# A delta-rule recurrence with an MLP behind it: chunks 0 and 1 solved apart, pairs from chunk 2 on, another split of the first tiles, and the order of the work from a table

## The chip, the cores and the metric

The kernel runs on one core of a Trainium2 chip. The metric is the device time of the program in microseconds (us). Its engines are PE (TensorE, matrix products, with its weight loads shown as PEld), DVE (VectorE), ACT (ScalarE), POOL (GpSimd) and SP (SyncE, which here only issues transfers). ACT and POOL issue transfers too.

## The reference

Each of 4 x 8 heads carries a state of 48 x 48 through 768 tokens. Its readings are put together to 384 columns, and an MLP with a tanh GELU runs over the 3072 tokens.

```python
def _attn_ref(q, k, v, beta):           # (4, 8, 768, 48); beta (4, 8, 768)
    k_n = k / (np.linalg.norm(k, axis=-1, keepdims=True) + 1e-06)
    state = zeros(B, H, D, D)
    for t in range(S):
        y[:, :, t] = einsum('bhd,bhde->bhe', q[:, :, t], state)
        v_old = einsum('bhde,bhd->bhe', state, kt)
        state = state + bt * einsum('bhd,bhe->bhde', kt, vt - v_old)

def _moe_ref(x, w_in, w_out):           # x (3072, 384), w_in (384, 2048), w_out (2048, 384)
    h = x @ w_in
    g = 0.5 * h * (1.0 + tanh(c * (h + 0.044715 * h**3)))
    return g @ w_out
```

## The kernel before

**The recurrence by chunks.** The 768 tokens are cut into 12 chunks of 64 (`C`, `NCH`). 32 heads lie as 16 pairs, a head in each half of the 128 partitions. Inside a chunk the recurrence is a triangular system: its matrix comes from the Gram matrix of the normalized keys times beta, and its inverse T, applied to v minus what the state already holds, gives the update U. The steps of a chunk `c` are:

- `load`: SP fetches keys, values and queries (`kf`, `vf`, `qf`; a chunk's keys are two transfers of 192 KB).
- `prep`, `prep2`, `prepq`: squares, sums and norms of the keys (`sq`, `ss`, `sr`, `rn`), the normalized keys `Kn`, and their transposes with the queries' in `KQT`, by PE with the identity as one operand.
- `gram`: the 64 x 64 products K K^T and K Q^T of every head; the first goes to `G`, the second, masked with `mD`, to `DT`.
- `own`, `blocks`: the diagonal 16 x 16 blocks of the triangular system. `own` makes the products of 32 x 32, a vector transpose puts them into `Tt`, they are multiplied with beta and a mask (`bM`) into `Y`, and 14 rounds of a multiplication and an addition each (28 instructions, `tmp` and `Y`) solve all blocks at once. Then beta goes in twice (`XW`), and vector transposes bring the results back as `TB`.
- `inverse`: `WB` and `DI` spread the solved blocks over the 64 columns, and four products with what follows each (`WB,G` to `ET`; then `DI,ET`, and `TT,ET` twice, each to a part of `TT`) build the whole inverse.
- `state`: KS (keys times state S) and R = KS - v; `R,TT` to U; KU to the next S; QS and DU to the output `x`.

A unit of two chunks shares one `blocks`: (0,1) is solved on DVE, and (2,3), (4,5) and on are solved on POOL (`UNITS`, `eng = "pool" if u else "dve"`). All of the solve is in f32.

**The MLP by tiles.** `TILES` are [0], [1], then [2,3], [4,5] to [10,11]. A tile with one chunk is 4 batches x 64 = 256 tokens, one with two is 512. Layer one has 16 blocks of 128 hidden columns, each the sum of three products with 128 rows of the weights `W1`. The 384 columns of x come out of `state` as 4 groups of 2 x 48 rows, so a gather of six small transfers (`x<-x`, issued by SP) moves the fourth group into free rows of the other three. Tile 0 does without the gather: it reads a fourth weight tile `W4` that lies for this time in the last four buffers of `gT`. ACT applies the GELU into `gT`; layer two is four groups of two bursts of 8 products each, whose result goes by `osb` to the output.

**What sets the order.** The kernel records operations (`P.op`) with the engines that may run them, an estimated cost, what they read and write, and a priority. `Plan.schedule` then simulates the engines, the transfers and the fetching of instructions (`Fetch`), and takes the ready operation of the best priority on each engine; it also gives out the eight PSUM banks. `Plan.emit` writes one instruction stream for each engine in that order, with semaphore waits where a dependency crosses engines. So every engine is in order, and an instruction that waits holds up all behind it on its own engine. The same holds for the transfers in SP's and POOL's queues.

Lines that the prediction's steps use: L372 is the helper of every tensor_tensor, L377 of copies, L381 of activations, L388 of matmuls, L396 of transfers; L897 is the transpose into `Tt`; L907, L912 and L916 the solve; L923 and L928 `XW`; L936 the transposes back; L979 `WB` and `DI`; L633 the memset for the fourth weight tile.

Of the kernel before, what the change touches and what calls it, by code (L numbers as in the profile page):

```python
# [5 lines left out]
F32 = mybir.dt.float32  # L6
BF16 = mybir.dt.bfloat16
# [7 lines left out]
LAT = {"pe": 0.22, "dve": 0.06, "act": 0.06, "pool": 0.08, "sp": 0.0}  # L15
SWITCH = 0.095
SLACK = 0.3
URGENT = -100.0
CRIT, WAIT = -85.0, 0.9
EARLY_T, MARGIN = 55.0, (2.0, 1.0, 0.2)  # L20
COLD_T, COLD = 36.0, 1.3
BURST = 1.2
BANKS = {"t": (0, 6), "f": (6, 8), "l": (0, 8)}
NEAR = {"pe": 0.3, "dve": 0.1, "act": 0.05, "pool": 0.1, "sp": 0.0}


def turn(a, b):
    if a == b:
        return 0.0
    return SWITCH  # L30


class Fetch:

    BLOCK, FIRST, EVENTS = 256, 63, 1.0025
    TIMES = ((50.0, 6.5), (125.0, 4.5), (1e9, 3.7))

    def __init__(self):
        self.pos, self.ready = float(self.FIRST), 0.0

    def run(self, t, cost, n, keep=False):
        pos, ready = self.pos, self.ready
        left = n * self.EVENTS
        per = cost / left
        while left > 1e-6:
            k = min(self.BLOCK - pos % self.BLOCK, left)
            t += k * per
            pos += k
            left -= k
            if self.BLOCK - pos % self.BLOCK < 1e-6:  # L50
                pos = float(round(pos))
            if pos % self.BLOCK == 0:
                t = max(t, ready)
                ready = t + next(w for x, w in self.TIMES if t < x)
        if keep:
            self.pos, self.ready = pos, ready
        return t


class Op:  # L60
    __slots__ = ("idx", "cost", "fns", "deps", "prio", "alloc", "uses", "dma", "lat",
                 "eng", "start", "end", "count", "clock", "sync", "mode", "bw", "bk", "fence", "nm", "at")


class Plan:


# [12 lines left out]
    def op(self, cost, fns, reads=(), writes=(), prio=0.0, alloc=(), dma=None, lat=0.0, mode="s", bk="t", bw=0.0, nm=0,  # L80
           free=(), at=0.0):
        o = Op()
        o.idx = len(self.ops)
        o.cost, o.fns, o.prio, o.dma, o.lat, o.mode, o.bw, o.bk, o.nm = cost, fns, prio, dma, lat, mode, bw, bk, 2 * nm
        o.alloc, o.at = tuple(alloc), at
# [29 lines left out]
    def schedule(self):  # L115
        ops = self.ops
        succ = [[] for _ in ops]
        left = [len(o.deps) for o in ops]
        for o in ops:
            for d in o.deps:  # L120
                succ[d].append(o.idx)
        ready = {e: [] for e in ENGINES}

        def push(o):
            for e in o.cost:
                ready[e].append(o.idx)

        for o in ops:
            if left[o.idx] == 0:
                push(o)  # L130
        free_at = {e: 0.0 for e in ENGINES}
        pe_mode = "s"
        burst = 0.0
        fetch = Fetch()
        dma_free = w_free = 0.0
        queued = []
        bank_free = [0.0] * self.nbanks
        bank_last = [()] * self.nbanks
        done = [False] * len(ops)
        orders = {e: [] for e in ENGINES}  # L140

        def dep_time(o, e):
            t = o.at
            for d in o.deps:
                p = ops[d]
                m = 0.0
                if o.prio > URGENT and p.end < EARLY_T and p.eng != e:
                    m = MARGIN[0] if p.dma else MARGIN[1] if p.eng == "pool" else MARGIN[2]
                t = max(t, p.end + m + (p.lat if p.dma else (0.03 if p.eng == e == "pe" else LAT[p.eng])))
            return t  # L150

        def find_banks(n, t0, lo, hi):
            best = None
            for i in range(lo, hi - n + 1):
                ts = bank_free[i:i + n]
                if any(x is None for x in ts):
                    continue
                t = max(max(ts), 0.0)
                key = (max(t, t0), i)
                if best is None or key < best[0]:  # L160
                    best = (key, i, t)
            return best

        n_left = len(ops)
        dep_cache = {}
        users_left = {h: len(u) for h, u in self.users.items()}
        while n_left:
            pick = None
            for e in ENGINES:
                if not ready[e]:  # L170
                    continue
                best = None
                for i in ready[e]:
                    o = ops[i]
                    if (i, e) not in dep_cache:
                        dep_cache[(i, e)] = dep_time(o, e)
                    t = max(free_at[e], dep_cache[(i, e)])
                    bb = []
                    tb = 0.0
                    if o.alloc:  # L180
                        ok = True
                        taken = []
                        for h, n in o.alloc:
                            sv = [(k, bank_free[k]) for k in taken]
                            for k in taken:
                                bank_free[k] = None
# [1111 lines left out]
```

## Time and profile before

| | us |
|---|---|
| runs | 259.02, 259.03, 259.76; median 259.03 |
| span of the profiled execution | 258.6 |
| PE busy | 216.8 (84%) |
| PE weight loads busy | 143.3 (55%) |
| DVE busy | 160.3 (62%) |
| ACT busy | 145.1 (56%) |
| POOL busy | 127.7 (49%) |
| moved by transfers | 24.56 MB, mean 95 GB/s |

A profile shows one execution. Busy time is the time in which an engine runs at least one instruction of the kind; matmuls overlap, and their ends are modelled. A group of instructions is told by its line, its engine, the operation and the tiles that it writes and reads. Idle time in front of an instruction is put down to what released it; "issue" means that nothing in the profile shows what it waited for. The granted clock is the share of full speed at which PE may run.

### The profile page before, as it was taken

The page shows a single profiled execution, that of the slowest core. Times are in us where ns is not written, and L with a number is a line of the kernel's source. Part 1 is how long each engine was busy: PE and PEld are TensorE (multiplying, and loading weights), DVE is VectorE, ACT ScalarE, POOL GpSimd, SP SyncE. Part 2 cuts the span into 40 slices and gives each one's busy share as a digit, 9 for nine tenths or more (in the row PEclk, how much of TensorE's full clock was granted, in tenths as well). Part 3 has the DMA queues.
Part 4 walks back from the last instruction along what each step waited for, and adds up shares of the span by engine and source line. Part 5 has one row for each costly group of instructions (what it writes and reads, how often), then busy time and mean ns, then how long its engine had stood idle before and what let it go on. Part 6 is the DMA issues. An engine that isn't in the chain of part 4 may idle for free.

```text
span 258.6 us, 11905 instructions
## 1 busy us (share of the span) xinstructions
PE 216.8 (84%) x5416; PEld 143.3 (55%) x5446; DVE 160.3 (62%) x288; ACT 145.1 (56%) x244; POOL 127.7 (49%) x234
## 2 busy tenths in 40 slices
PE   0573455559998789999989989999999999999995
PEld 0352345547875676555656655656556554446462
DVE  5659777683857999986998679738976210001011
ACT  4587895226954776379830578732676506850600
POOL 8559998989058892789518860686000000000000
PEclk9999995556999979999999999999999999999999
DMA  7999799981298855840611404131100030002111
GB/s 131 209 159 220 139 180 169 193 159 37 51 167 195 202 111 111 186 86 23 124 48 67 96 17 81 35 74 63 56 18 5 3 109 30 0 3 82 39 49 72
DMA packets 66129, 24.56 MB, mean 95 GB/s; under 512 B 53216, under 2 KB 65600, under 8 KB 66080
## 3 DMA queue, kind: packets, MB, share of 16 engines
q1 hardware_dynamic: 58368, 15.26, 31.1%
q0 software_dynamic: 2752, 3.54, 8.8%
q10 hardware_dynamic: 4960, 5.02, 5.7%
q8 instruction: 42, 0.69, 1.2%
q14 instruction: 7, 0.06, 0.1%
HBM read 21.43 MB, written 4.72 MB: 101 GB/s over the span
## 4 chain that ended last, share of the span: by engine, by line
PE 41%; POOL 28%; DVE 15%; issue 4%; DMA 4%; SPq 3%; ACT 3%; POOLq 0%
PE ps L388 40%; POOL Yf L916 6%; POOL tmp L912 6%; POOL Kn L372 4%; POOL sq L372 4%; SPq L396 3%; POOL W L396 3%; DMA qf<-in_q_dram 2%; DVE TB L936 2%; DVE WB L979 2%; DMA kf<-in_k_dram 2%; POOL DT L372 2%; POOL Yf L907 1%; ACT gT L381 1%; DVE TT L372 1%
## 5 line engine op out<-in xcount | busy, mean ns | idle before, releaser
L381 ACT ACTIVATE gT<-ps 128x512 bf16<-128x512 f32 x96 | 55.6, 597 | 40.0 <-PE ps L388 37.9
L388 PE MATMUL ps<-x,W 128*128 128x512 bf16 (+1 forms) x306 | 67.4, 353 | 4.5 <-issue 2.5
L388 PE MATMUL ps<-W,gT 128*128 128x384 bf16 x384 | 66.9, 327 | 0.0
L388 PEld LDWEIGHTS ps<-W,gT 128*128 128x128 bf16 x384 | 35.8, 98 | 23.8 <-ACT gT L381 0.5
L377 DVE COPY osb<-ps 128x384 f32<-128x384 f32 x21 | 11.7, 556 | 53.8 <-PE ps L388 53.7
L388 PEld LDWEIGHTS ps<-x,W 128*128 128x128 bf16 x336 | 29.9, 99 | 24.6 <-ACT gT L381 1.0
L372 DVE TENSOR_TENSOR TT<-ps,DI 128x256 bf16<-128x256 f32 (+4 forms) x39 | 24.9, 644 | 13.1 <-PE ps L388 12.6
L381 ACT ACTIVATE KQT<-ps 128x1024 bf16<-128x1024 bf16 (+1 forms) x24 | 23.6, 984 | 12.9 <-PE ps L795 10.6
L916 POOL TENSOR_TENSOR Yf<-Yf,tmp 128x28 f32<-128x28 f32 (+6 forms) x70 | 24.6, 351 | 5.5
L912 POOL TENSOR_TENSOR tmp<-Yf 128x28 f32<-128x28 f32 (+6 forms) x70 | 23.8, 340 | 5.4
L388 PE MATMUL ps<-KQT 48*32 48x32 bf16 (+1 forms) x1152 | 20.1, 207 | 6.8 <-DVE tmp L912 2.9
L381 ACT ACTIVATE G<-ps 128x512 bf16<-128x512 f32 x24 | 14.2, 595 | 16.8 <-PE ps L388 16.7
L388 PEld LDWEIGHTS ps<-KQT 48*32 48x32 bf16 (+1 forms) x1152 | 15.1, 102 | 12.4 <-ACT KQT L381 5.3
L388 PEld LDWEIGHTS ps<-TT,ET 64*64 64x64 bf16 x768 | 15.8, 117 | 10.5 <-issue 7.2
L372 POOL TENSOR_TENSOR Kn<-kf,rn 128x768 bf16<-128x768 f32 (+1 forms) x12 | 17.0, 1429 | 8.9 <-DVE rn L737 7.0
L388 PE MATMUL ps<-TT,ET 64*64 64x32 bf16 (+1 forms) x768 | 17.9, 182 | 4.2 <-issue 4.1
L381 ACT ACTIVATE x<-ps 128x1024 bf16<-128x1024 f32 x12 | 12.3, 1021 | 6.9 <-PE ps L388 6.6
L795 PE MATMUL ps<-identB,Kn 128*128 128x128 bf16 x96 | 10.1, 265 | 6.4 <-POOL Kn L372 5.0
L841 DVE TENSOR_TENSOR DT<-ps,mD 128x512 bf16<-128x512 f32 x20 | 13.5, 677 | 2.8 <-ACT G L381 2.7
L936 DVE STREAM_TRANSPOSE TB<-XW 128x512 f32<-128x512 f32 x12 | 12.4, 1047 | 4.2 <-POOL XW L928 4.2
L372 DVE TENSOR_TENSOR ET<-ps,mE 128x768 bf16<-128x768 f32 (+1 forms) x13 | 11.5, 888 | 3.6 <-PE ps L388 3.6
L381 ACT ACTIVATE U<-ps 128x768 bf16<-128x768 f32 x12 | 9.7, 807 | 6.0 <-PE ps L388 6.0
(100 smaller groups left out, 309.1 us busy)
## 6 DMA issues: line engine op xcount, KB each, us to landing
qf<-in_q_dram SPq DMA_DIRECT2D x24, 192.0 KB, 4.0
kf<-in_k_dram SPq DMA_DIRECT2D x23, 192.0 KB, 4.6
vf<-in_v_dram SPq DMA_DIRECT2D x40, 96.0 KB, 3.4
out_dram<-osb ACTq DMA_DIRECT2D x20, 192.0 KB, 1.8
W<-in_moe_w_in_dram POOLq DMA_DIRECT2D x8, 192.0 KB, 7.1
W<-in_moe_w_out_dram POOLq DMA_DIRECT2D x4, 384.0 KB, 13.6
vf<-in_v_dram SPq DMA_DIRECT2D x4, 192.0 KB, 5.5
out_dram<-osb ACTq DMA_DIRECT2D x8, 96.0 KB, 3.8
```

The lines of the kernel that those rows point to most:

```text
L372: return lambda e: e.tensor_tensor(out() if callable(out) else out, a() if callable(a) else a, b() if callable(b) else b, op)
L377: return lambda e: e.tensor_copy(out, a() if callable(a) else a)
L381: return lambda e: e.activation(out, a() if callable(a) else a, func)
L388: ins = t.matmul(out, lhsT, rhs, start=st, stop=sp_, skip_group_check=skip)
L396: return lambda e: e.dma_start(out, a)
L795: ins = e.transpose(tb()[:, m, :], t[:, 2 * m:2 * m + 2, :].rearrange("p h d -> p (h d)"), identB[:, :])
L841: op(d_ps(512), {"dve": lambda e: e.tensor_tensor(dv, gview(1)(), md, ALU.mult)}, reads=[h] + MD, writes=[dn], prio=dp)
L907: sb_op(256 * nb, lambda e: e.tensor_tensor(Yv(), tv_, bm, ALU.mult), [f"Tt{j}", bmn], [YN], 0, [(hY, 1)] if inp else ())
L912: sb_op(nb * s * w, lambda e, s=s, w=w, tv=tv: e.tensor_tensor(tv, yf[:, :, s:s + 1, 0:s].to_broadcast([128, nb, w, s]), Yv()[:, :, s + 1: ...
L916: sb_op(nb * s * w, lambda e, s=s, tv=tv: e.tensor_tensor(Yv()[:, :, s + 1:16, 0:s], Yv()[:, :, s + 1:16, 0:s], tv, ALU.add), [YN, f"tmp{j ...
L936: op({"dve": 1.05}, {"dve": lambda e, w=w: e.transpose(TB1.rearrange("q (n j) -> q j n", j=16) if w else TB0[:, 0:2, :].rearrange("q s (x ...
L979: return e.tensor_tensor(o_.rearrange("q p (b j) -> q p b j", j=16), i_.unsqueeze(2).to_broadcast([128, n_, 3, 16]), mB[:, 16 - 16 * w:64 ...
```

## The change

- **Units.** `UNITS` is now [0], [1], [2,3], [4,5] and on. Chunk 0 is solved alone on DVE, chunk 1 alone on POOL, by a new function `blocks_one` at half the width (256 columns in place of 512); pairs from (2,3) on stay on POOL. For chunks 0 and 1 beta is prepared apart (`pat`, `sel`, `btd`, `btz`), by DVE.
- **Type of the solved blocks.** `XW`, `TB1` and `TB0` are bf16 in place of f32. The rounds of the solve stay in f32.
- **Tiles.** `TILES` is [0], [1], [2], [3], then [4,5] and on. The fourth weight tile, its memset, its two transfers and its matmuls are gone; tile 0 is gathered like the others.
- **Early steps.** Chunk 1's keys are taken in one part, chunks 2 and 3 have their sums of squares by one DVE reduction in place of a tree on POOL, `DT` of chunks 0 and 1 is masked by DVE straight from PSUM in place of an ACT copy and a POOL product, `inverse` of chunk 1 goes by two halves like chunk 0's, and U and x of chunks 0 and 1 are split in two. More copies may run on either of DVE and ACT. `BL` lies in the place of the last `osb`.
- **Weights.** The loads of `W1` wait for the first queries in place of the first keys.
- **Order.** The simulating scheduler, its costs and its priorities are gone. A table `ORDER` lists every operation with its engine in one sequence, and `BANK` lists the PSUM bank of every product; `schedule` reads both. `emit` is as before.

```diff
-class Fetch:
+ORDER = """
+v32 a45 g12 s44 v41 g20 v2 g21 a47 s46 v7 g13 v8 g17 a27 s48 v0 v43 a1 g18 v6 v42 s49 g19 v33 v38 g10 v34 v35 s51 v36
...
+BANK = ("601210010046030303033653...
...
+        for n, w in enumerate(ORDER.split()):
+            o = ops[int(w[1:])]
+            o.eng, o.end = names[w[0]], n
...
-    TILES = [[0], [1]] + [[c, c + 1] for c in range(2, NCH, 2)]
+    TILES = [[0], [1], [2], [3]] + [[c, c + 1] for c in range(4, NCH, 2)]
...
-        UNITS = [[2 * u, 2 * u + 1] for u in range(NU)]
+        UNITS = [[0], [1]] + [[c, c + 1] for c in range(2, NCH, 2)]
...
-        XW = [sb(f"XW{j}", [128, 16, 2, 16], F32) for j in range(2)]
-        TB1 = sb("TB1", [128, 512], F32)
-        TB0 = sb("TB0", [128, 3, 256], F32)
+        XW = [sb(f"XW{j}", [128, 16, 2, 16], BF16) for j in range(2)]
+        TB1 = sb("TB1", [128, 512], BF16)
+        TB0 = sb("TB0", [128, 3, 256], BF16)
...
+        WAFT = [f"qf_{b}" for b in range(B)]
...
-            after = ["kf0_0", "kf0_1"]
+            after = WAFT
...
-                if c in (2, 3):
-                    for z in (24, 12, 6, 3):
-                        op({"pool": ...}, {"pool": f_tt(sq[:, :, 0:z], sq[:, :, 0:z], sq[:, :, z:2 * z], ALU.add)}, ...
+                op({"dve": 0.95 * w}, {"dve": lambda e, u=u: e.tensor_reduce(ss[j][:, u], sq[:, u, :], AX.X, ALU.add)},
...
+        def blocks_one(c):
+            h = own([c])
+            eng = "pool" if c else "dve"
...
+            op({"dve": 0.75}, {"dve": lambda e: e.transpose(
+                Tt[c][:, 0:512].rearrange("q (x y) -> q x y", y=32),
+                banks2(h)[:, :, 0:256].rearrange("q h (n x) -> q x n h", x=16))},
...
+            op({"pool": 1.25} if c else {"dve": 0.95}, {eng: f_tt(tc, tc, bM[c], ALU.mult)}, ...
+            op({"pool": 0.65} if c else {"dve": 0.43}, {eng: f_tt(yf[:, 0], tc[:, 0], tc[:, 1], ALU.add)}, ...
...
+            solve(eng, Yv, yf, tmp[c], 1, YN, f"Y{c}", f"tmp{c}")
...
-            nk = KT if t else 4
-            wn = (W1N if t else W1N + W4N + W4S)
+            nk, wn = KT, W1N
```

## The prediction

> **What bounds the kernel now.** I read the slices first, then a table of stages, then the order of time on PE, POOL and VectorE (DVE).
>
> ```profile
> PE   0573455559998789999989989999999999999995
> PEclk9999995556999979999999999999999999999999
> DMA  7999799981298855840611404131100030002111
> ```
>
> A slice is 6.47 us. PE is about half busy in the first nine (58 us) and nearly full from there to the end; its granted clock is halved in slices 6 to 9. The stages (PE, weight load, DVE, ACT, POOL, clock, DMA, GB/s):
>
> ```profile
> 39.60:56.50 16.90, 9.57 (x379) 8.82 (x379) 12.61 (x27) 5.96 (x8) 14.64 (x34) 0.50 1.16 172
> 56.50:62.40 5.90, 5.45 (x102) 3.52 (x98) 2.19 (x3) 2.04 (x4) 5.90 (x6) 0.53 0.33 89
> 62.40:80.00 17.60, 17.48 (x548) 13.45 (x537) 11.97 (x17) 12.64 (x20) 8.19 (x16) 1.00 0.55 112
> 80.00:100.00 20.00, 17.07 (x450) 13.18 (x448) 19.59 (x32) 14.55 (x23) 15.38 (x25) 0.91 0.73 156
> 100.00:204.50 104.50, 99.43 (x3219) 63.48 (x3244) 80.06 (x126) 62.16 (x98) 51.64 (x104) 1.00 0.27 64
> 204.50:258.60 54.10, 50.84 (x292) 27.19 (x280) 6.70 (x12) 19.04 (x33) 0.00 (x0) 1.00 0.13 46
> ```
>
> From 62.4 us PE idles 11.4 us of 196.2: PE is the bound there, and time is won by doing its work earlier. Until then a chain of latencies rules. The timelines of PE, POOL and DVE (start, duration; in brackets the idle time before):
>
> ```profile
> 39.56 0.46 PE L388 MATMUL ps<-DI,ET 64*64 64x48 bf16 x10 [2.83 <-issue]
> 47.26 1.31 PE L388 MATMUL ps<-TT,ET 64*64 64x16 bf16 x43 [4.12 <-issue]
> 53.16 0.37 PE L388 MATMUL ps<-DT,U 64*64 64x64 bf16 x11 [2.31 <-issue]
> 56.50 0.82 PE L388 MATMUL ps<-x,W 128*128 128x256 bf16 x3
> 66.70 0.44 PE L388 MATMUL ps<-WB,G 64*64 64x48 bf16 x32
> ...
> 1.99 1.80 POOL L633 MEMSET gT<- 128x2048 bf16 x1
> 31.50 3.28 POOL L396 DMA_DIRECT2D W<-in_moe_w_in_dram  x6
> 34.77 1.02 POOL L396 DMA_DIRECT2D gT<-in_moe_w_in_dram  x2
> 36.84 3.04 POOL L396 DMA_DIRECT2D W<-in_moe_w_out_dram  x4
> 56.51 1.50 POOL L923 TENSOR_TENSOR XW<-Yf,nbT 128x512 f32<-128x512 f32 x1
> ...
> 2.00 2.12 DVE L377 CAST identB<-identF 128x128 bf16<-128x128 f32 x1
> 16.99 1.25 DVE L897 STREAM_TRANSPOSE Tt<-ps 128x1024 f32<-128x1024 f32 x1 [1.77 <-PE ps L388]
> ```
>
> Chunks 0 and 1 wait for each other at 16.99 though chunk 0's products ended at 11.82. The first MLP matmul stands at 56.50. Three gaps (9.26 us) are waits for nothing that shows, while the weights issued from 31.5 to 39.9 land. The mark I use below is E, the product WB,G of chunk 2, the first fruit of the second solve: 66.70.
>
> **The change, by its parts.** After E the new order is PE-bound too: per pair of chunks POOL has 1.29 + 11.9 (28 solve steps, 75.4 to 87.3) + 1.31 + 2 x 1.48 + 0.8 + 1.5 + 2.57 = 22.3 us, PE 216.8 / 6 = 36. So new span = 258.6 - (PE work done before E that now comes after it) + (new E - 66.70) - (idle time lost later).
>
> *Work pulled ahead of E.* In the new table's PE order these stand before E, and after 66.70 now, each from start to next start at full clock: tile 0's last six blocks of layer one, 6 x 0.435 = 2.61; three of four bursts of its layer two, 3 x 1.32 = 3.96 (64 matmuls in 10.57); K5's transposes 0.5; own blocks of 4 and 5, 0.59 + 0.69; Q's transposes 0.90; three halves of Gram matrices 1.2; the first block of tile 1, 6 x 0.109 = 0.65. That is 11.1. Behind E go KU of chunk 1 (0.27) and KS and QS of chunk 2 (0.64). Net 10.2. The six blocks include the fourth weight tile's matmuls; splitting tile (2,3) costs nothing: 96 matmuls at 0.109 for 48 at 0.217 (1.24 for 5 plus gap), with a weight load of 98 ns under each, and 12 more small x<-x issues on SP, which idles; were the loads bare it were 96 x 0.098 = 9.4 us, but the 256-wide rows already run at 0.109 beside them.
>
> *Chunk 0, to its first MLP matmul.* Transpose Tt at 12.3 instead of 16.99 (own blocks done 11.9, DVE until then on norms of chunk 1 and the new small beta operations). Half width: Tt 0.65, times bM 0.9 (between 0.69 and 1.43), two adds 0.8, 28 steps 6.5 (rows 0.18 at 28 elements to 0.28 at 112, so 0.176 to 0.219 at 14 to 56, sum 5.7, and 0.03 between); put among them chunk 1's Tt 0.65 and a reduction 0.93; then 0.1, XW 0.6, back transpose 1.05: 24.5, where TB was ready at 32.0. Bf16 blocks are in no row; 1.05 is the f32 transpose, half of it the other bound, 0.5 each either way, and I take the f32 row, since the element counts are the same. Then WB on ACT (2.17 for six of them) 26.6, ET on ACT 28.8, three rounds of product and TT (0.43 + 0.52, 0.45 + 0.45, 0.3 + 0.3) and the DT products (now DVE 0.68 for ACT 0.60 and POOL 1.16) to 32.1, U 33.2, x 35.3. Now TB to U takes 18.3, of which 6.95 are the first two gaps: the same pace. SP then issues six x<-x for tile 0, which the fourth tile spared: 3.92 and 2.0 to land, behind chunk 5's kf loads that wait for K2 on DVE: 41.3, against 56.50.
>
> *Chunk 1 and the pair (2,3) on POOL.* POOL loses the memset 1.80, two issues 1.02, the reduction trees of chunks 2 and 3 (6.3; DVE takes them as 0.93 each), four DT products (4.6) and K2; 384 KB of weights less to move, 2.2 us at 173 GB/s. It gains chunk 1. Five W1 issues now stand from 12 us ahead of bM1 and K1, so K1 ends at 17.5, own(1) at 20.0, Tt1 at 20.8. From there: product and add 1.29 + 0.65, 28 half-width steps 9.8 (0.22 to 0.30, and 0.08 between), K3 1.48, memset 0.15, two W1 issues 1.1, XW 1.51 and 1.06, two bM 2.62, four W2 issues 3.08: 43.5. The pair's Tt is ready at 44.0; 1.29 + 11.9 + bM 1.31 + K4 and K5 2.96 + 0.15 + XW 1.51: 63.1, where the same step ends at 58.0 now. TB 1.05 and WB 0.96: 65.1. K4 waits for norms that DVE ends near 52: up to 2 more.
>
> *E by PE's own load.* Between 41.3 and E the order holds 18.2 us (tile 0: 5.2 + 4.0; tile 1's block 0.65; rest 8.4). The clock came back 5.9 us after dense work began (56.50 to 62.40), so 2.9 more; waits for chunk 1's DI (at 45) and TT 4: 66.4. I take E = 67. Low bound 64 (bf16 at half price); high bound 76 (all 9.26 us of gaps return; nearer zero, since no weights are issued from 18 to 34).
>
> Copies of KQT, U and x that go from ACT to DVE (0.42 for 512 columns, 0.95 for 768) lie beside PE's work after E, where DVE is busy 80 of 104 us; were that cover gone, chunks' state chains would slow and not PE, until the stored MLP work (51 us at 204.5) is used up. BL in osb3's place costs nothing: osb3 is first written after E.
>
> *Idle later.* 80 to 100 us loses 2.9 idle and about 1.4 to the clock, while chunks 2 and 3 come through; the new order has 15 blocks of tile 1 (9.9 us) ready behind E. Between 0 and 4.3; I take 2.1.
>
> Sum: 258.6 - 10.2 + 0.3 - 2.1 = 246.6. The profiled run's span is 258.6 and the median of the runs 259.03; with the 0.4 between them, **247.0 us**.
>
> **Two rules of the Trainium skill.** "SBUF — State Buffer", section "Who interferes with whom", says that VectorE's copies, casts and tensor_scalars can take a port pair shared with GpSimd for a whole instruction, and that operations with two SBUF inputs collide with GpSimd's reads. The cast of identB agrees: 2.12 us for 128 columns while POOL's memset ran 1.80. It speaks against six tensor_scalar DI beside POOL's solve; at a wait of 0.45 for each, 2.7 us, the sum were 249.7 if that reached E. "TensorE: Matmul & The Clock Gate", section "What's actually happening", gives about 3.4 us of sustained work before the full clock, where the rows show 5.9; by it PE's load would end 1.2 earlier, at 65.2, and the sum were 0.2 to 1.8 less.
>
> **Rivals.** (A) *The early weights crowd the loads.* Six W1 transfers of 192 KB now go out at 12 to 18 us beside vf0, kf2 and kf3; at 173 GB/s that is 6.6 us. For it: DMA share is 0.94 to 1.26 to 58 us. Against: they wait for the first q, so only vf0 is still missing for chunk 0. If all of it reaches E: 247.0 + 6.6 = 253.6.
> (B) *POOL becomes the bound before E.* PE is in order, and fifteen blocks of tile 1 stand behind WB,G. POOL's stretch from 20.8 to 63.1 is 42.3 us; each 10% is 4.2 us at the end. It decides once E passes 66.7 + 10.2 + 2.1 = 79.0, a stretch by a third, from DVE taking the shared memory paths. For it: WB<-TB,mB takes 0.92 to 2.22 us. Against: POOL's own rows hardly vary (XW 1.50 to 1.52). At a half, E = 86, 266 us.
> (C) *It only moves idle time.* The work pulled ahead leaves a hole before pair (4,5); 10 us lost there, 259. Against: 22 us on POOL a pair for 36 on PE.
>
> **How the numbers follow.** Forecast 0.66 (243 to 251), A 0.20 (251 to 256), C 0.04, B 0.10. The time is 247.0. The low end is E at 64 (-3.0), all 4.3 of idle (-2.2) and some 2 of the 5.1 idle from 100 to 204: 240; the high end E at 76: 256. What a measurement tells from no change is about 0.3%, 0.8 us: faster 0.86, same 0.03, slower 0.11.
>
> **What would show it.** Right: Tt of chunk 0 near 12.3, x near 35, the first x,W near 41 with tile 0's second layer before E, E near 67, PE over 95% busy from there. Wrong: "issue" gaps of several us before 41; E past 72 behind XW on POOL; K1 waiting behind weight issues past 18; new holes in PE after 90.

## The result, and the profile after

The changed kernel took **274.6 us** (median; 274.54 to 274.61) where the kernel before took 259.02 on the same chip: a ratio of 1.0593, 95% interval 1.0575 to 1.0611. The forecast was 247.0 with a range to 256. The span of its profiled execution is 272.8. Below, a time in us is the median of a kernel's runs, while a ratio and its interval leave out runs more than 1.5% above the fastest of their kernel, so the two need not agree (e1: median 268.35, but 266.3 over the runs in its ratio).

The slices of the changed kernel (6.82 us each), to be read against those of before:

```profile
PE   0541178569978894899979699999999999999995
PEclk9999999655899998699999889999999999999999
DMA  8999937995453674842301400315120111011012
```

Counted from 1, the clock falls in slices 8 to 11 and again in 16 and 17 (to 0.6), where before it fell in 7 to 10 (the prediction's 6 to 9, counted from 0) and in 15; the end is as dense as it was. The clock is not what costs the time: the four runs had mean granted clocks of 0.944 to 0.975 and took 274.54 to 274.61 us. PE is thin in the first nine slices, and has holes up to slice 23. The shares of the chain that ended last, first of the kernel before, then of the changed one:

```profile
PE 41%; POOL 28%; DVE 15%; issue 4%; DMA 4%; SPq 3%; ACT 3%; POOLq 0%
```

```profile
PE 49%; DVE 32%; DMA 4%; POOL 4%; SPq 4%; ACT 3%; issue 2%; POOLq 0%
```

POOL has left the chain, as planned, and DVE has come in its place. PE's timeline of the changed kernel at the marks that the prediction named (start, duration, in brackets the idle time before):

```profile
26.42 0.69 PE L257 MATMUL ps<-KQT 48*32 48x32 bf16 x64 [8.02 <-ACT KQT L250]
...
33.92 0.62 PE L257 MATMUL ps<-WB,G 64*64 64x48 bf16 x16 [5.18 <-ACT WB L841]
...
54.12 1.25 PE L257 MATMUL ps<-x,W 128*128 128x256 bf16 x5
...
82.30 0.44 PE L257 MATMUL ps<-WB,G 64*64 64x48 bf16 x32 [1.53 <-DVE WB L850]
```

E, the product WB,G of chunk 2, stands at 82.30 and not at 67, and the first MLP matmul at 54.12 and not at 41.3. The first line is the product `own` of chunk 1, forecast to end at 20.0. DVE and POOL of the changed kernel:

```profile
13.53 0.42 DVE L241 TENSOR_TENSOR Yf<-Tt 128x256 f32<-128x256 f32 x1
13.87 3.74 DVE L765 TENSOR_TENSOR ps<-Tt 128x256 f32<-128x256 f32 x1
...
27.33 0.72 DVE L756 STREAM_TRANSPOSE Tt<-ps 128x512 f32<-128x512 f32 x1 [3.97 <-PE ps L257]
...
30.52 2.32 DVE L740 STREAM_TRANSPOSE TB<-XW 128x512 bf16<-128x512 bf16 x1
...
53.13 2.44 DVE L740 STREAM_TRANSPOSE TB<-XW 128x512 bf16<-128x512 bf16 x1
55.20 1.42 DVE L799 STREAM_TRANSPOSE Tt<-ps 128x1024 f32<-128x1024 f32 x1
```

```profile
25.86 1.46 POOL L241 TENSOR_TENSOR sq<-kf 128x768 f32<-128x768 f32 x1 [8.04 <-DMA kf<-in_k_dram]
...
28.13 1.27 POOL L241 TENSOR_TENSOR Tt<-Tt,bM 128x512 f32<-128x512 f32 x1 [0.82 <-DVE Tt L756]
...
56.71 1.28 POOL L241 TENSOR_TENSOR Yf<-Tt,bM 128x512 f32<-128x512 f32 x1 [4.39 <-DVE Tt L799]
```

A single wait runs through four engines here. ACT's R of chunk 0 waited 7.67 us for `vf` and began at 24.12. Behind it in ACT's order stood the copy of chunk 1's KQT (25.35), behind that on PE `own` of chunk 1 (26.42), behind that on DVE chunk 1's Tt (27.33), and behind that, again on DVE, the last two rounds of chunk 0, which needed nothing of chunk 1. Later DVE is the late one without waiting: the pair's Tt stands in a full queue, right behind a back transpose of 2.44 us.

The stages after, first of the kernel before and then of the changed one, cut at the first WB,G of each pair (span, busy time and count on PE, weight load, DVE, ACT, POOL, then clock, DMA share, GB/s):

```profile
66.70:102.54 35.84, 32.79 (x993) 24.90 (x993) 29.50 (x46) 24.05 (x35) 22.69 (x39) 0.95 0.68 143
...
188.21:258.60 70.39, 66.34 (x858) 37.06 (x865) 15.95 (x24) 29.96 (x52) 0.00 (x0) 1.00 0.11 38
```

```profile
82.30:122.96 40.66, 33.66 (x954) 25.36 (x958) 37.08 (x55) 24.89 (x43) 26.20 (x47) 0.92 0.56 122
...
208.61:272.80 64.19, 61.28 (x922) 34.89 (x907) 18.14 (x25) 22.68 (x39) 0.00 (x0) 1.00 0.12 42
```

In the first pair's march after E (a march is the stretch from one pair's first WB,G to the next pair's) DVE is busy 37.08 of 40.66 us (91%) and PE 33.66 (83%): DVE is the fullest engine there, PE was before. The tail behind the last pair's WB,G fell from 70.4 to 64.2, so work did move ahead of E, but the four marches took 126.3 us in place of 121.5 (all of it in the first, 40.66 for 35.84; the three behind it took 85.65 for 85.67) and E came 15.6 later: 15.6 + 4.8 - 6.2 = 14.2, which is the difference of the spans.

### The profile page after: what moved, and what is told of

Same layout as the page of the kernel before. It is cut to its first block, busy times and chain, and to the rows that moved or that the text cites. A ratio compares the mean times of both kernels' runs of the same rounds, so it can differ in the third digit from the quotient of the medians.

```text
span 272.8 us, 12077 instructions
## 1 busy us (share of the span) xinstructions
PE 222.8 (82%) x5478; PEld 149.2 (55%) x5478; DVE 190.6 (70%) x324; ACT 143.8 (53%) x263; POOL 119.4 (44%) x241
## 4 chain that ended last, share of the span: by engine, by line
PE 49%; DVE 32%; DMA 4%; POOL 4%; SPq 4%; ACT 3%; issue 2%; POOLq 0%
PE ps L257 48%; DVE TB L740 12%; DMA vf<-in_v_dram 4%; SPq L265 4%; DVE TT L241 2%; POOL Yf L733 2%; DVE ss L574 2%; POOL tmp L730 2%; DVE DI L850 2%; DVE DT L690 2%; DVE nw L241 1%; PE ps L651 1%; DVE R L241 1%; DVE ET L241 1%; DVE Tt L799 1%
## 5 line engine op out<-in xcount | busy, mean ns | idle before, releaser
L257 PE MATMUL ps<-x,W 128*128 128x256 bf16 (+1 forms) x384 | 76.1, 343 | 2.5 <-issue 1.9
L257 PEld LDWEIGHTS ps<-W,gT 128*128 128x128 bf16 x384 | 36.1, 98 | 24.5 <-DVE osb L246 0.6
L257 PEld LDWEIGHTS ps<-x,W 128*128 128x128 bf16 x384 | 35.7, 102 | 24.7 <-issue 2.5
L740 DVE STREAM_TRANSPOSE TB<-XW 128x512 bf16<-128x512 bf16 x14 | 33.6, 2399 | 1.4 <-POOL XW L241 1.3
L257 PE MATMUL ps<-KQT 48*32 48x32 bf16 (+1 forms) x1152 | 18.9, 208 | 16.3 <-ACT KQT L250 9.8
L733 POOL TENSOR_TENSOR Yf<-Yf,tmp 128x28 f32<-128x28 f32 (+13 forms) x84 | 28.7, 341 | 6.1
L730 POOL TENSOR_TENSOR tmp<-Yf 128x28 f32<-128x28 f32 (+13 forms) x84 | 27.9, 332 | 6.1
L241 POOL TENSOR_TENSOR Kn<-kf,rn 128x768 bf16<-128x768 f32 (+1 forms) x11 | 16.1, 1467 | 17.0 <-DVE rn L600 7.8
L250 ACT ACTIVATE KQT<-ps 128x1024 bf16<-128x1024 bf16 (+1 forms) x16 | 15.5, 970 | 10.6 <-PE ps L651 5.3
L250 ACT ACTIVATE osb<-ps 128x384 f32<-128x384 f32 x11 | 5.4, 489 | 27.1 <-PE ps L257 27.1
L257 PE MATMUL ps<-WB,G 64*64 64x48 bf16 x384 | 6.9, 194 | 10.5 <-ACT WB L841 5.4
L841 ACT ACTIVATE WB<-TB,mBs 128x256 bf16<-128x256 bf16 (+1 forms) x27 | 10.6, 461 | 8.7 <-DVE TB L740 5.9
L574 DVE TENSOR_REDUCE ss<-sq 128x16 f32<-128x768 f32 (+1 forms) x13 | 11.2, 871 | 4.3 <-ACT sq L250 4.3
```

The costliest lines, as they stand in the source:

```text
L241: return lambda e: e.tensor_tensor(out() if callable(out) else out, a() if callable(a) else a, b() if callable(b) else b, op)
L250: return lambda e: e.activation(out, a() if callable(a) else a, func)
L257: ins = t.matmul(out, lhsT, rhs, start=st, stop=sp_, skip_group_check=skip)
L574: op({"dve": 0.95 * w}, {"dve": lambda e, u=u: e.tensor_reduce(ss[j][:, u], sq[:, u, :], AX.X, ALU.add)}, reads=[f"sq{n}"], writes=[f"ss{j ...
L730: sop(nb * s * w, lambda e, s=s, w=w, tv=tv: e.tensor_tensor(tv, yf[:, :, s:s + 1, 0:s].to_broadcast([128, nb, w, s]), Yv()[:, :, s + 1:16 ...
L733: sop(nb * s * w, lambda e, s=s, tv=tv: e.tensor_tensor(Yv()[:, :, s + 1:16, 0:s], Yv()[:, :, s + 1:16, 0:s], tv, ALU.add), [YN, TN], [YN])
```

## The experiments

Three theories stood at the start. (1) *The bf16 blocks*: the back transposes went from 1.05 us to 2.40, and DVE became the bound. (2) *The start*: waits in in-order queues (R on ACT, `sq` of chunk 2 on POOL) hold up chunk 1. (3) Rival A of the prediction, *the early weights crowd the loads*. Each run below is one of the two kernels, or an earlier run, with the edit shown, and its ratio is to the kernel before on the same chip.

**Type and place, alone and together.** e1 puts `XW`, `TB1` and `TB0` back to f32, e4 makes them bf16 in the kernel before (its planner left as it is), e2 moves one operation in the table, e3 does both e1 and e2.

```diff
-        XW = [sb(f"XW{j}", [128, 16, 2, 16], BF16) for j in range(2)]
-        TB1 = sb("TB1", [128, 512], BF16)
-        TB0 = sb("TB0", [128, 3, 256], BF16)
+        XW = [sb(f"XW{j}", [128, 16, 2, 16], F32) for j in range(2)]
+        TB1 = sb("TB1", [128, 512], F32)
+        TB0 = sb("TB0", [128, 3, 256], F32)
```

```diff
-... v164 a216 v165 ...  p317 a318 v180
+... v164 v165 ...  p317 a318 a216 v180
```

> The changed kernel with the solved blocks and their transposed copies back in f32, and nothing else. Theory 1 (the bf16 back transpose on VectorE costs 2.4 us where the f32 one cost 1.05): the back transposes fall to about 1.05 us each, VectorE's busy time from 190.6 by 14 x 1.35 = 19 us to about 172; of the 33 us that this line has on the chain of waits some 15 to 19 come back: 256 to 260 us. Theory 2 (the start is late, because the early weight loads crowd the first v tile, for which ScalarE waits with chunk 1's key copy queued behind): only the two transposes of chunk 0 and one of the pair come back, 270 to 273 us. Theory 3 (the new order itself, whatever the type): 272 us or more.

> The changed kernel with one instruction moved: ScalarE's negated copy of v of chunk 0 (R) goes behind chunk 1's key copy and the G copies, so that these no longer wait for the v tile. Theory 2: chunk 1's own product at about 18 to 19 us instead of 26.4, GpSimd's chain some 7 us earlier, and with it the product WB,G of chunk 2 at about 75 instead of 82.3: 266 to 268 us. Theory 1: the start gains the same 7 us, but VectorE's slow transposes hold the middle, so that at most 4 of them reach the end: 270 to 274 us.

> Both edits: blocks in f32, and the copy of v behind chunk 1's key copy. Theory 1 and 2 as independent terms: 256 to 260 less 4 to 8, so 249 to 255 us, below the kernel before (259.0). If one of the two carries everything, no more than 1 us below the better of the two single edits.

> The kernel before with that part alone: solved blocks and their transposed copies in bf16, order and everything else as before. Theory 1: each of the 12 back transposes takes about 2.4 us instead of 1.05, 16 us more on VectorE (160 to 176 of 259); six pairs of 2.7 us more, some of which VectorE's idle time takes up: 262 to 270 us. If the slow transposes of the changed kernel come from its order (what runs beside them), they stay near 1.05 here and the time within 1 us of 259.

| | time, us | ratio to before (95%) | E, us |
|---|---|---|---|
| changed kernel | 274.6 | 1.059 (1.058 to 1.061) | 82.30 |
| e1, f32 | 268.35 | 1.028 (1.019 to 1.038) | 79.28 |
| e2, R later | 272.69 | 1.053 (1.047 to 1.060) | 78.76 |
| e3, both | 266.33 | 1.031 (1.024 to 1.038) | 79.05 |
| e4, before with bf16 | 264.85 | 1.023 (1.019 to 1.027) | 65.86 |

The groups of the back transposes (count, busy time, mean ns, then idle time before), in the changed kernel, e1 and e4:

```profile
L740 DVE STREAM_TRANSPOSE TB<-XW 128x512 bf16<-128x512 bf16 x14 | 33.6, 2399 | 1.4 <-POOL XW L241 1.3
```

```profile
L740 DVE STREAM_TRANSPOSE TB<-XW 128x512 f32<-128x512 f32 x14 | 14.7, 1050 | 2.4 <-POOL XW L241 2.4
```

```profile
L936 DVE STREAM_TRANSPOSE TB<-XW 128x512 bf16<-128x512 bf16 x12 | 28.7, 2427 | 3.4 <-POOL XW L928 3.4
```

The type alone costs 5.8 us in the kernel before, and its return gives back 3.1 points of ratio (2.0 to 4.2 by the intervals), about 8 us, in the changed one. DVE's busy time fell from 190.6 to 179.9 in e1 and not by the 18.9 that the transposes gave up, because the readers of bf16 blocks are the cheaper ones (DI 504 ns for 708, WB 602 for 1062). In e4 E came 0.8 us *earlier* than before, at 65.86, and what follows took 196.9 for 191.9: there the price falls after E. Theory 1 holds in kind, and not in size: e1 was expected at 256 to 260 us, and e3 at 249 to 255, below the kernel before, yet e3 is no better than e1. The two edits do not add, in the time or in E.

e2 did to its place what it should, brought E 3.5 us forward and did nearly nothing to the time. PE and POOL of e2:

```profile
19.51 0.69 PE L253 MATMUL ps<-KQT 48*32 48x32 bf16 x64 [1.11 <-ACT KQT L246]
```

```profile
26.18 1.46 POOL L237 TENSOR_TENSOR sq<-kf 128x768 f32<-128x768 f32 x1 [8.37 <-DMA kf<-in_k_dram]
```

`own` of chunk 1 came 6.9 us earlier, but on POOL its solve stood behind `sq` of chunk 2, whose keys landed at 26.18 as ever: one wait gave its place to the next.

**The early weights, and the rest of the start.** e5 is e3 with the five early W1 issues put behind K1. e6 is e5 with `sq` of chunk 2 behind chunk 1's sum on POOL, and with what needs that `sq` further back on DVE and ACT. e8 is e6 with the three tensor_scalar WB that DVE had moved to ACT. e14 is e8 with three W2 issues later.

```diff
 e5
-... a90 g71 v152 s89 g73 a91 ... p92 g72 g69 s104 ... v154 g74 s142 ... g101 p192
+... a90 v152 s89 a91 ... p92 s104 ... v154 s142 ... g101 g71 g73 g72 g69 g74 p192
 e6
-... g110 v173 ... v111 g279 ... a118 g280 ... a112 g282 a113 ... v188 a196 ... a201 v119 ... a203 g294 v197
+... v173 ... g279 ... g280 g110 ... g282 ... v188 v111 a196 ... a201 ... a203 a118 a112 a113 g294 v197 v119
 e8
-s232 v321 a320 s231
+s232 a320 a321 s231
 e14
-v316 g138 a390 s356 v313 g140 p453 a326 s355 p349 g139 ... g423 v398
+v316 a390 s356 v313 p453 a326 s355 p349 ... g423 g138 g140 g139 v398
```

> The run with both edits (blocks in f32, copy of v behind the key copy; 266.3 us) and five of the six early weight issues on GpSimd moved some 6 us, from ahead of K of chunk 1 to behind it, where GpSimd stood idle. Theory A (the early weight transfers crowd the k and v loads that SP issues from 12 to 24 us; 5 x 192 KB at about 175 GB/s are 5.6 us): kf of chunk 2 lands at 20 to 22 us instead of 26, GpSimd's chunk-1 solve starts 4 to 6 us earlier, TB of chunk 0 is ready at 27 to 29 instead of 32.7, and E (WB,G of chunk 2) falls from 79 to 74 to 76: 262 to 264 us. Rival (SP's issues are held up by the loads' own volume or by other waits): kf still lands at 25 to 26, 266 us.

> As the run before in this list, and the squares of chunk 2 on GpSimd with the reduction behind them on VectorE moved behind the start of chunk 1's solve and the end of chunk 0's, with the norms that follow on ScalarE. In-order theory (both solves wait in their engine's queue for a load they don't need): GpSimd starts chunk 1's solve at 21 to 22 us whatever lands when, TB of chunk 0 ready at about 27, E at 72 to 74: 260 to 262 us. Rival (E is set by VectorE's later work and by PE's own load): E no earlier than 77, 265 us or more.

> As e6, and one of the two WB copies of chunk 1 moved from VectorE (three tensor_scalars that took 3.65 us beside two GpSimd products, where six others of the same size took 1.4) to ScalarE, which idled. Port theory (VectorE's tensor_scalar is held up while GpSimd reads or writes SBUF): the transpose Tt of the pair (2,3) starts about 3 us earlier, and E with it: 2 to 3 us below e6. Rival (Tt waits for other work on VectorE or for PE's own products): within 1 us of e6.

> As e8, and the last three weight issues of the second layer moved on GpSimd from ahead of the pair's solve into it, 5 to 6 us later. Crowding theory (rival A of the prediction, at its second place): the x<-x copies of tile 0 land at 48 to 49 instead of 52.5 us and the first x,W product follows at once; GpSimd's chain of the pair starts up to 1.6 us earlier and then loses 2.3 to the issues, so E moves by less than 1: the end stays within 1 us of e8, because nothing before E is bound by PE. If PE's load before E counts, 2 to 4 us less.

SP's own queue of issues in the changed kernel, and in e5:

```profile
13.17 10.55 SPq L265 DMA_DIRECT2D kf<-in_k_dram  x3
```

```profile
13.13 4.76 SPq L261 DMA_DIRECT2D kf<-in_k_dram  x3
17.93 9.99 SPq L261 DMA_DIRECT2D vf<-in_v_dram  x3
```

e5 took 265.28 us (1.022; 1.016 to 1.027). With the weights later the keys of chunk 2 did not land earlier: POOL began `sq` at 27.89, after 9.85 us of waiting. A stretch of some ten us in which SP's queue does not get on moved from the keys to the values, and stayed. But e5 does not decide against rival A, because it moved the five issues by only 3 us: all six now stand from 14.75 to 18.04, where they stood from 11.82 to 17.81. The traces speak for A. The transfer queues from 13 to 28 us (packets, MB, share of the engines), q1 with SP's loads and q0 with POOL's weights, in the kernel before, the changed one and e5:

```profile
q1 hardware_dynamic: 10749, 2.61, 102.2%
```

```profile
q1 hardware_dynamic: 7692, 1.45, 63.7%
q0 software_dynamic: 384, 1.18, 43.0%
```

```profile
q1 hardware_dynamic: 7070, 1.33, 82.0%
q0 software_dynamic: 384, 1.18, 43.3%
```

Between 13 and 28 us the transfers move 2.65 MB at 177 GB/s in the kernel before and the same in the changed one, and what the weights take of it the loads lack. In e5 the loads thin out later, as the weights come later: 0.85 MB from 13 to 20 us where the changed kernel has 0.39, then 0.48 where it has 1.06. No run kept the weights out of that stretch, so what the crowding costs at the end stays open.

e6 took 264.72 us (1.017; 1.010 to 1.024) and brought the start close to where the prediction had it: chunk 1's sum on POOL at 23.24, the first back transpose of chunk 0 done at 24.5. And still E is at 76.97. DVE of e6 tells why:

```profile
41.47 1.05 DVE L736 STREAM_TRANSPOSE TB<-XW 128x512 f32<-128x512 f32 x1 [1.44 <-POOL XW L769]
42.56 3.93 DVE L853 TENSOR_SCALAR WB<-TB,mBs 128x128 bf16<-128x128 f32 x3
46.12 0.68 DVE L242 COPY KQT<-ps 128x1024 bf16<-128x1024 bf16 x1
46.72 0.94 DVE L237 TENSOR_TENSOR R<-ps,vf 128x768 bf16<-128x768 f32 x1
47.58 0.94 DVE L570 TENSOR_REDUCE ss<-sq 128x16 f32<-128x768 f32 x1
48.44 0.67 DVE L686 TENSOR_TENSOR DT<-ps,mD 128x512 bf16<-128x512 f32 x1
49.04 1.05 DVE L736 STREAM_TRANSPOSE TB<-XW 128x512 f32<-128x512 f32 x1
49.95 1.19 DVE L795 STREAM_TRANSPOSE Tt<-ps 128x1024 f32<-128x1024 f32 x1
```

Eight lines with hardly a gap: the pair's Tt is seven places back in a queue of moved copies, reductions and masks. e8 took the largest of them off; Tt then came at 48.60, after a wait of 0.79 for PE, E came at 76.31, and the time stayed (264.58; 1.017, 1.011 to 1.023). In e14 the load in front of the first MLP matmul came 4.2 us earlier, as PE of e8 and of e14 show:

```profile
52.56 1.46 PE L253 MATMUL ps<-x,W 128*128 128x256 bf16 x6 [3.06 <-DMA x<-x]
```

```profile
48.31 1.25 PE L253 MATMUL ps<-x,W 128*128 128x256 bf16 x5
```

E came 0.8 earlier (75.50), and the time got worse (267.89; 1.030, 1.026 to 1.034). The weights did crowd that load, but having it earlier gains nothing; what the issues cost in their new place, inside the pair's solve, was not told apart.

**Other parts alone, in the kernel before.** e7 splits the tile (2,3), e9 gives DVE the sums of squares of chunks 2 and 3. In both the kernel's planner makes a new order for it.

```diff
 e7
-    TILES = [[0], [1]] + [[c, c + 1] for c in range(2, NCH, 2)]
+    TILES = [[0], [1], [2], [3]] + [[c, c + 1] for c in range(4, NCH, 2)]
 e9
-                if c in (2, 3):
+                if False:
```

> The kernel before with the chunks 2 and 3 as two MLP tiles instead of one, nothing else (its planner orders the rest anew from there on). The prediction's step (splitting costs nothing): 258.5 to 259.5 us, or less if the earlier tile fills PE's idle time. The other reading of the rows (96 matmuls of 256 columns at 0.153 to 0.163 us each for 48 of 512 at 0.245): 2.9 to 3.8 us more PE time, 261 to 263 us.

> The kernel before with one other part of the change alone: the norms of chunks 2 and 3 are summed by one reduction each on VectorE (0.93 us) instead of trees on GpSimd (6.3 us in all), on whose chain they lie with the weight issues behind them; blocks in f32, one solve for chunks 0 and 1, the tile of chunks 2 and 3 whole. If GpSimd's queue before the pair's solve is what sets E there (as the prediction counted it), the weights are issued 4 to 6 us earlier, the solve starts at 36 instead of 39.9 and E falls from 66.7 to 63 to 65: 255 to 258 us. If PE's own load sets E, or VectorE's reductions delay chunk 0's solve by as much: 258.5 to 261 us.

e7: 265.78 us (1.021; 1.015 to 1.028). e9: 267.36 (1.034; 1.025 to 1.043), although its E is at 61.29, 5.4 earlier. Both are above all that was expected of them (up to 263 and 261). So the formula "new span = 258.6 - work before E + (new E - 66.70)" fails as a tool by itself: an earlier E under another order is no shorter kernel. Since the planner moves much else, the order had to be held still.

**The same with the order held.** e16 is the kernel before with its own order written out as a table, and with the output copies and issues placed as early as they can be; e15 is e16 with the tile split; e17 is the kernel before, its order kept as a table, with the reductions of e9.

> The control: the kernel before with its own order written down as a table, the tile of chunks 2 and 3 whole; only output copies stand as early as they can. 258.5 to 260 us.

> The kernel before with the order that its planner makes written down as a table, chunks 2 and 3 split into two MLP tiles, and the tiles' matmuls put into the same places of PE's order (every other operation keeps its place; six more x<-x copies on SP). The prediction's step (the split costs nothing on PE): within 1 us of the control with the whole tile. The other: 48 x (2 x 0.153 - 0.245) = 2.9 us more on PE and the waits for the second tile's copies, 3 to 6 us more than the control.

> The kernel before with its own order written down, and the norms of chunks 2 and 3 summed by one reduction on VectorE each in place of the trees on GpSimd; every other operation keeps its place. If E counts (the prediction's formula: new span = old span + (new E - old E)), E falls by 2 to 5 us and the span by as much: 254 to 257 us. If the pace after E is set by VectorE's chain and the loads and not by E, the gain is below half of what E gains; if the fetch gaps from 39 to 53 us grow since the weights now go out beside the loads, nothing is left: 258 to 262 us.

e16 took 282.63 us (1.091; 1.082 to 1.100) and e15 287.7 (1.108; 1.103 to 1.113): the split costs 5.1 us at a fixed order, if in a kernel 9% slower, and 6.6 us in e7. The layer one matmuls by shape, e16 and then e15 (busy us, mean ns):

```profile
L310 PE MATMUL ps<-x,W 128*128 128x512 bf16 x240 | 59.5, 381 | 0.4 <-ACT gT L303 0.2
L310 PE MATMUL ps<-x,W 128*128 128x256 bf16 x96 | 16.1, 305 | 0.0
```

```profile
L310 PE MATMUL ps<-x,W 128*128 128x512 bf16 x192 | 48.1, 386 | 0.4 <-ACT gT L303 0.2
L310 PE MATMUL ps<-x,W 128*128 128x256 bf16 x192 | 29.2, 291 | 0.0
```

77.3 us in place of 75.6: only 1.7 of the 5.1 are PE's own work. For the rest there is one row in e8: between 95.9 and 103.25 the gather of tile 3 (x on ACT, six issues on SP, 1.79 us to land) is in the chain. But PE has other work for most of it: of its idle time there a TT of DVE ended 2.14 us and the gather 0.44. So what the remainder is was not shown.

e17 took 259.87 us (1.001; 0.998 to 1.005). With the order held the reductions bring E 1.4 us forward (65.27) and gain nothing; POOL's weight issues still begin at 31.87 (31.50 before), whatever POOL is spared ahead of them.

e16 itself was meant as a control, expected at 258.5 to 260, and is a result: hardly more than the places of the output copies and issues (of PE's 316 operations nine stand elsewhere than in e17's table) costs 9%. Two of its waits (us in all, times, longest):

```profile
DVE osb L299 <- PE ps L310: 71.1, 20, 14.5
...
ACT KQT L303 <- DVE osb L299: 11.4, 1, 11.4
```

An output copy that stands early in DVE's queue waits for late MLP work on PE, and a copy of the recurrence waits for it.

**The changed kernel with the tile whole.** e10 is e8 with the tile (2,3) joined, in a table made by rule; e11 the same with the MLP spread evenly, and e13 its partner with the tile split and the same spread.

> As e8 (264.6 us), but chunks 2 and 3 as one MLP tile again, as in the kernel before; the table is e8's with the MLP's matmuls of that tile put into its later MLP places, what doesn't fit going to the end. It has the single solves of chunks 0 and 1 in f32, without the bf16 blocks and without the split. If the split is what PE's idle time after E comes from (as the kernel before with the split alone, 2.1% slower, suggests): 257 to 261 us. If the idle time comes from VectorE's queue in front of the products of the pairs: 263 to 267 us.

> As e8 (264.6 us), with chunks 2 and 3 as one MLP tile, and the MLP's matmuls spread evenly behind the other products on PE (one after each second product up to that tile, three after each four from there), since the table of e10 starved PE (it put the tile's work at the end). The split theory: with e13, which has the same placing and the tile split, this one is 3 to 6 us shorter. The rival (the split costs nothing, as the prediction had it): within 1.5 us of e13.

> As e8, tiles split as in the changed kernel, and the MLP's matmuls spread by the same rule as in e11: the control for it. By itself it tells what the placing in the new table is worth against an even spread: 264 to 270 us if the spread is no better, 258 to 262 if the holes without MLP work in the table (five and then fifteen products of chunks 4 and 5 with none between) are what PE idles in.

294.83, 330.22 and 332.92 us. The last two differ by 2.7 us, with runs that overlap (325.5 to 333.6 and 330.4 to 334.5). Over the two shorter runs of e11 the whole tile would be some 5 us the better, as in e16 against e15, but with that spread nothing is told apart. What they show is the price of a poor table, 30 to 68 us, more than any part of the change.

**Why the bf16 transpose is slow.** `TB1` is written with 16 elements between neighbours. e18 (from the changed kernel, bf16) and e19 (from e8, f32) write it in order and let the readers stride.

```diff
-                TB1.rearrange("q (n j) -> q j n", j=16) if w else
+                TB1.rearrange("q (j n) -> q j n", j=16) if w else
...
-        TBV = {1: TB1.rearrange("q (c p j) -> q c p j", c=2, j=16), ...
+        TBV = {1: TB1.rearrange("q (j c p) -> q c p j", c=2, j=16), ...
...
-            return {1: (TB1.rearrange("q (m c p j) -> q c m p j", m=8, c=2, j=16), ["TB1"]),
+            return {1: (TB1.rearrange("q (j m c p) -> q c m p j", m=8, c=2, j=16), ["TB1"]),
```

> The changed kernel (bf16 blocks), with the back transpose of one of the two blocks (TB1, 7 of the 14) written in order, 32 elements side by side, instead of one element each 16; the readers WB take it with a stride instead. If the 2.4 us come from writing 2-byte elements 32 bytes apart, these 7 fall to 1.2 us or less, the other 7 stay at 2.4, VectorE's busy time falls by 8 us less what WB's reads lose, and the time by 2 to 4 us: 270 to 272.5. If bf16 itself makes the transpose slow, all 14 stay at 2.4 and the time at 274.6.

> e8 (blocks in f32, 264.6 us) with the same block written in order. If the order of writing sets the price in f32 too, these 7 fall from 1.05 us toward the 0.71 us that the transpose of 512 columns from PSUM into consecutive places takes, 2.4 us of VectorE's time: 263 to 264.5. If not, they stay at 1.05 and the time at 264 to 265.5.

DVE of e18 and of e19; in each the first line writes `TB1` in order, the second `TB0`, left as it was, with its neighbours apart:

```profile
77.28 0.67 DVE L740 STREAM_TRANSPOSE TB<-XW 128x512 bf16<-128x512 bf16 x1
...
79.87 2.48 DVE L740 STREAM_TRANSPOSE TB<-XW 128x512 bf16<-128x512 bf16 x1
```

```profile
73.11 0.67 DVE L736 STREAM_TRANSPOSE TB<-XW 128x512 f32<-128x512 f32 x1
...
75.72 1.08 DVE L736 STREAM_TRANSPOSE TB<-XW 128x512 f32<-128x512 f32 x1
```

In order both types take 0.67; with the stride bf16 takes 2.48 and f32 1.08. So it is the order of writing, and it weighs far more on two-byte elements. The readers pay for it: WB of 128x768 on DVE went from 1065 ns in e8 to 1634 in e19 and from 602 to 1612 in e18, WB on ACT from 498 to 730. e18 took 272.04 us (1.040; 1.030 to 1.050) and e19 268.35 (1.028; 1.020 to 1.036): a gain for bf16, none for f32.

No version run beats the kernel before; e17 equals it.

## Why the prediction was wrong, point by point

The span missed its forecast by 272.8 - 246.6 = 26.2 us: 15.3 up to E (82.30 for 67) and 10.9 behind it (190.5 for 179.6).

- **"Half width: Tt 0.65 ... 24.5" (chunk 0).** Tt stood at 12.05 (forecast 12.3), the back transpose began at 30.52 (24.5 with its end). Two terms failed. "Two adds 0.8" took 0.42 + 3.74: the second ran beside POOL's bM and K1, and in e5, beside K1, it was 1.58 + 0.42. In e1 and e18 the first was the long one (3.92, 3.88); in all of them it ends 0.3 us behind K1. And chunk 1's Tt, "put among them" at 0.65, came with a wait of 3.97 for a PE product that had not been made. With the table's start mended, e6 met the 24.5. The first x,W behind it (54.12 for 41.3) was late by x (44.85 for 35.3) and by its six issues (5.73 for 3.92); e14 shows that having it earlier gains nothing.
- **"own(1) at 20.0, Tt1 at 20.8".** K1 ended at 17.31 (17.5), so the sign that I had named for rival A did not show; the term that failed is the step behind it, 28.13 for 20.8. I had followed chunk 1 on POOL and PE, and not the queue of ACT, where R of chunk 0 waited for `vf` ahead of the copy that `own` needs. In the changed kernel's chain that is 7.3 us. e2 moved it and found the next wait, `sq` on POOL; only e6, with both gone, had the product at 21.89, and its E is 5.3 us earlier, with f32 in it. `vf` and the keys behind it were late beside 1.18 MB of weights, about 6.7 us at 177 GB/s as an estimate, which is rival A's mechanism and nearly its price (6.6); how much of it reached the end was not run.
- **"The pair's Tt is ready at 44.0".** The product came at 56.71; beyond the 7.3 that is another 5.4, of which POOL idled 4.39. The step took PE and the norms into account and not DVE's queue: three bf16 back transposes of 2.3 to 2.4 us, the moved copies, and WB at 1.48. In e6 this queue holds E at 77 even in f32; in e8 Tt waits for PE, and E is at 76.3.
- **"1.29 + 11.9 + ..., 63.1" (the pair's solve).** Right: 19.1 us from the product to the end of the XW that E needs (74.29 + 1.51). Rival B, POOL as the bound, did not come. From there to E it was 6.5 us for 3.9: the back transpose stood until 79.32 in DVE's queue, behind norms, an output copy and the next pair's Tt, and then took 2.33.
- **"Bf16 blocks are in no row; 1.05 is the f32 transpose, half of it the other bound".** The main failure. I bounded it by 0.5 either way "since the element counts are the same"; it is 2.30 to 2.49, outside the bound, in all fourteen. The row of f32 already held the strided write (0.67 in order), so it was no bound for another type. Alone this is 5.8 us (e4) to about 8 (e1). The Trainium skill, "VectorE: DVE Perf Modes", section "The three transpose paths", gives 311 ns for a 128x128 transpose of bf16 on VectorE, 1.24 us by its rate for 512 columns, as an estimate. The rows here are 0.67 in order and 2.4 strided; the measurement decides, and the page's figure goes with neither.
- **"Copies ... lie beside PE's work after E, where DVE is busy 80 of 104 us; were that cover gone, chunks' state chains would slow and not PE".** The cover was gone, DVE at 91% of the march, and PE did slow: after E it waited 6.0 us for TT and 3.5 for ET, both from DVE (2.8 and 3.5 in e1). Its idle time was forecast 2.1 lower and came 3.5 higher: 5.6 us of the miss, and about a third of the 10 us lost that rival C had put there.
- **"Net 10.2" of work pulled ahead.** PE's work after E fell by 4.9, from 180.52 to 175.66: 5.3 of the miss. The trace of before lacks 30 of 336 x,W matmuls, so the cut between work and idle time is rough; their sum, 10.9, is not.
- **"Splitting tile (2,3) costs nothing".** It costs 1.6 to 2.1% (e15 against e16; e7), 1.7 us of it on PE. The other bound that I named, weight loads laid bare at 9.4, is not it; whether the additional gather is a part was not shown.
- **"+ (new E - 66.70)".** That a us of E is a us at the end is the first step of the sum, and it does not hold from one order to another: e9, e14 and e17 have E earlier by 5.4, 0.8 and 1.4 than the kernels that they start from, and none is faster.
- **Right:** the gaps that showed as "issue" on PE are nearly gone (1.9 us over the span for 12.2), and from the end of the back transpose to U chunk 0 nearly keeps its pace (9.8 us for 8.7).
- **The rule on ports.** The prediction priced "SBUF — State Buffer", section "Who interferes with whom", at 0.45 for each of six tensor_scalar DI. Those six took 1.08 us in all. What was long was elsewhere: an add of two SBUF operands, 3.74 for 0.42, and perhaps the three tensor_scalar WB of e6, 3.93 us beside two POOL products, where six DI of the same shape and type took 0.68 + 0.62; that POOL is the cause there was not tested. The place was wrong and the size too small.

By the parts measured, bf16 is worth about 6 to 8 us, the split about 4 to 6, and the start's order and weights about 3 to 4 (e3 to e8, 1.031 to 1.017, with intervals that just fail to touch): some 13 to 18, for 15.6. These come from different kernels, and that they add was not shown. No run had f32, the whole tile, chunks solved apart and a good table together. So whether solving chunks 0 and 1 apart gains anything by itself stays open.

## What to carry to other kernels

Moving work off the engine in the chain only helps if the one that takes it is not dense at that place: add up its busy share in that very stage with the moved work in, not over the span. In an order by table, follow each step through every queue that it crosses and ask what waits ahead of it; a wait moved away tends to uncover the next, here ACT's R, then POOL's `sq`, then DVE. A change of type needs its own row for each access pattern, since the same element count in a narrower type may cost more than double.

## What the runs showed of the hardware

- A vector transpose of 128x512 takes 0.67 to 0.71 us when it writes in order, in f32 and bf16. Written with 16 or more elements from one to the next it takes 1.05 to 1.08 in f32 and 2.3 to 2.5 in bf16, so the narrower type is the slower.
- Of two 128x256 f32 adds of the same operands on DVE one took 0.42 us and the other, beside POOL's tensor_tensors, 3.74 (changed kernel, the one that writes to PSUM), 3.92 (e1, the one that writes to SBUF) or 1.58 (e5, beside K1 alone).
- Between 13 and 28 us the transfers move 177 GB/s before and after the change (169 in e5), and what POOL's weights take of it SP's loads lack: 2.61 MB of loads with no weights (before), 1.45 beside 1.18 MB of weights (changed kernel). SP's queue stands there for some ten us at three issues of 96 to 192 KB, in the changed kernel at the keys and in e5 at the values.
- In e16 48 layer one products of 512 columns took 11.4 us of PE (59.5 - 48.1), and the 96 of 256 columns that took their place in e15 13.1 (29.2 - 16.1): two halves cost 15% more busy time than a whole.
